# A block of linear attention and SwiGLU: the outputs' way back in halves, another round with one SwiGLU unit, centring a round later

## The chip, the cores and the metric

The kernel runs on one core of a Trainium2 chip. The metric is the device time of one execution in microseconds. Several executions give a median; one more was recorded by the hardware profiler, and all engine and queue times below are from that one.

The core has five engines, each with its own instruction queue in order: TensorE (PE in the profile, its weight loads PEld), VectorE (DVE), ScalarE (ACT), GpSimd (POOL) and SyncE (SP). In this kernel SP issues every DMA, so SP's queue decides when each transfer starts. PSUM, where TensorE leaves its results, has eight banks; here six turn in a ring and two form one pair.

## The reference

```python
xn = layernorm(x)                                   # x: 2048 tokens x 640, bf16
q, k, v = split(xn @ wqkv)                          # 32 heads of 20
pq, pk = q @ w_phi, k @ w_phi                       # per head
phi_q = concat(softmax(pq), softmax(-pq))           # 40 features per head
phi_k = concat(softmax(pk), softmax(-pk))
kv, z = phi_k^T @ v, sum over tokens of phi_k       # per head
o = (phi_q @ kv) / (phi_q @ z + 1e-6)
out = x + o @ wo + (silu(xn @ w1) * (xn @ w3)) @ w2 # SwiGLU width 1536
```

`kv` and `z` are sums over all tokens, so K's stage must be complete before any `o` can be made.

## The kernel before

The tokens are 16 tiles of 128, and four groups of four tiles. The program's order is written out by hand and kept; each engine takes its instructions in that order.

**First stage (to about 58 us).** Tiles are loaded, normalized and transposed into `xnT` (features on partitions, tokens along), weights are loaded, `w_phi` is multiplied into the K and Q projections (`fuse`), and `v` is computed (`vaug`). For the first four tiles (`RAW = 4`) v is computed from x that is not centred; it is corrected later: `column_sum` (L334, ScalarE) sums the columns of v's weights, the sums go out to `row` in DRAM and come back on all partitions (`less_sum`, in the tile `wide`), and `raw_centred` (L342, VectorE) adds drift times sum to `v_raw` and writes `vaug`.

**K's stage.** A loop of 16 rounds over the tiles, the four uncentred ones last. A round has `phi_unit` (TensorE's `pk`; exponentials on ScalarE; row sums L422 and reciprocals L424 on VectorE; the product L425 on GpSimd), `kv_unit` for the tile of two rounds before (TensorE's `pkv`), and one or two SwiGLU units from a list (`fill`: `gp` and `up` on TensorE, a tanh on ScalarE, the products L489 and L492 on VectorE, into `hT`). The condition on `i` names the rounds with one unit. Rounds 4 to 8 also have a `fuse` and a `column_sum`; round 9 issues `row` and `less_sum`; rounds 10 to 13 have a `raw_centred`.

**Q's stage.** A loop of 20 rounds `t`. Rounds 0 to 15 have `phi_unit` for Q (`pq`), and `phi_transposed(t)` (L528) issues the DMA transpose of its phi into one of two buffers. Two rounds later `r_unit(t - 2)` (L537, `pr`) multiplies it by `kv`, VectorE divides (L553 to L558), and `o_transposed` (L583) issues the DMA transpose of the result. Rounds 0 to 6 fill with the rest of the SwiGLU units.

The output of groups 0 to 2 is made transposed: `out_piece(g, c)` makes 128 features for 512 tokens (12 matmuls L642 and 5 L647, one bank), and VectorE adds x transposed (L650) and writes `yTs[g % 2]`. `x_back(t)` (L632) issues the DMA transpose of a tile of x from DRAM for it, into `xTs[g]`; groups 0 and 2 share one buffer. `group_back(g)` (L656) transposes a group's output by DMA into the only buffer `y`, and `group_stored(g)` stores `y`. The last group's four tiles are made the other way round, with tokens on partitions (`out_unit`, L600; 34 matmuls for a tile, and for the last tile two parts of 17); each takes a row block of x (`residual`, two buffers `xr`), adds it (L609) and stores the result.

In each round of Q's loop SP is given, in this order: what `out_unit` and `residual` issue, `o_transposed`, `phi_transposed`, `group_back`, `group_stored`, `x_back`. In round 12 all engines also load a flag (L974) that chooses whether a safe second computation follows; here it does not run. SP waits at each of its instructions until what this one needs is there, and all behind it wait with it.

Of the kernel before, what the change touches and what calls it, by code (L numbers as in the profile page):

```python
# [8 lines left out]
P = 128  # L9
# [3 lines left out]
def kernel(  # L13
# [33 lines left out]
    RAW = 4  # L47
# [12 lines left out]
    out2 = out[0]  # L60
# [6 lines left out]
    def bank(name, dt=f32):  # L67
        n = 512 if dt == f32 else 1024
        return psum.tile([P, n], dt, name=name, tag="bank")

    def pair(name):
# [43 lines left out]
    yTs = [  # L115
        a.rearrange("p (t c s) -> p t c s", t=4, c=KD)
        for a in (flat1[:, 0:G], flat3[:, 2 * G : 3 * G])
    ]
    y = flat1[:, G : 2 * G].rearrange("p (t c s) -> p t c s", t=4, c=KD)
# [25 lines left out]
    def ld(dst, src):  # L145
        nc.sync.dma_start(out=dst, in_=src)
# [9 lines left out]
    with tc.manual_schedule():  # L156
# [18 lines left out]
        for c in range(KD):  # L175
# [15 lines left out]
            out=mask[:], in_=mask[:], pattern=[[-20, LH]], base=0,  # L191
# [3 lines left out]
            out=mask[:], in_=mask[:], pattern=[[20, LH]], base=19,  # L195
# [7 lines left out]
            out=own[:], in_=own[:], pattern=[[-64, 2], [-20, 3]], base=0,  # L203
# [3 lines left out]
            out=own[:], in_=own[:], pattern=[[64, 2], [20, 3]], base=19,  # L207
# [124 lines left out]
        def column_sum(c):  # L332
            junk = work.tile([P, D], bf, name="junk")
            nc.scalar.activation(  # L334
                out=junk[:], in_=wvT[:, c], func=AF.Identity, scale=-1.0,
                accum_out=sums[:, c : c + 1],
            )

        def raw_centred(t):
            for c0, n, k in ((0, 10, 60), (10, 1, 40)):  # L340
                cols = slice(60 * c0, 60 * c0 + k * n)
                nc.vector.scalar_tensor_tensor(  # L342
                    out=vaug[:, t, c0 : c0 + n, 1 : 1 + k],
                    in0=less_sum[:, cols].rearrange("p (c e) -> p c e", c=n),
                    scalar=drift[:, t : t + 1],
                    in1=v_raw[:, t, cols].rearrange("p (c e) -> p c e", c=n),
                    op0=ALU.mult, op1=ALU.add,
                )

        def tile_of(t):  # L350
            return slice(t * P, (t + 1) * P)
# [61 lines left out]
        def phi_unit(t, w, name, exps=exps, cols=None):  # L413

            ps = by_token(cols or tile_of(t), w, name, CH)
            dst = phi[:, t % 4]
            exps(ps, dst)
            rows = dst.rearrange("p c g f -> p (c g) f")[:, :, 0:60].rearrange(
                "p a (i d) -> p a i d", d=Dh
            )  # L420
            sk = work.tile([P, 2 * NCH, 3], f32, name="sk")
            nc.vector.reduce_sum(out=sk[:], in_=rows, axis=AX.X)  # L422
            rk = work.tile([P, 2 * NCH, 3], f32, name="rk")
            nc.vector.reciprocal(out=rk[:], in_=sk[:])  # L424
            nc.gpsimd.tensor_mul(  # L425
                out=rows, in0=rows, in1=rk[:, :, :, None].to_broadcast([P, 2 * NCH, 3, Dh])
            )
# [12 lines left out]
        def fuse(dst, wT, d, ps, copy=None):  # L440

            for c in range(NF):
                b, i = divmod(c, 3)
                h0 = 4 if c == NF - 1 else 0
                nc.tensor.matmul(
                    ps[b][:, FR * i : FR * i + Dh * (LH - h0)],
                    wT[0:FR, c, d * P : (d + 1) * P],
                    wphi[0:FR, c, h0:LH],
                    start=(i == 0),
                    stop=(i == 2),  # L450
                    skip_group_check=True,
                )
            nc.scalar.copy(out=dst[:, d, 0:CH], in_=ps[0][:, 0:CH])
            (copy or nc.scalar.copy)(out=dst[:, d, CH:D], in_=ps[1][:, 0 : D - CH])
# [43 lines left out]
        def kv_unit(t, v1, acc, first, last):  # L498

            for c in range(NCH):  # L500
                b, i = divmod(c, 6)
                nc.tensor.matmul(  # L502
                    acc[:, b, VC * i : VC * i + 1 + Dh * HC[c]],
                    phi[:, t % 4, c].rearrange("p g f -> p (g f)"),
                    v1[:, c, 0 : 1 + Dh * HC[c]],
                    start=(first and i == 0),
                    stop=last,
                    skip_group_check=True,
                )
# [120 lines left out]
        def x_back(t):  # L630
            g, j = divmod(t, 4)
            nc.sync.dma_start_transpose(  # L632
                out=xTs[g][:, :, j * P : (j + 1) * P], in_=x2[tile_of(t), :]
            )
# [17 lines left out]
                in1=xTs[g][:, c].rearrange("p (t s) -> p t s", t=4), op=ALU.add,  # L652
            )

        def group_back(g):
            nc.sync.dma_start_transpose(  # L656
                out=y.rearrange("p t c s -> p (t c) s"),
                in_=yTs[g % 2].rearrange("p t c s -> p (t c s)"),
            )

        def group_stored(g):
            rows = out2[4 * g * P : 4 * (g + 1) * P, :]
            ld(rows.rearrange("(t p) d -> p t d", p=P), y.rearrange("p t c s -> p t (c s)"))

        norms = one.tile([P, 8], f32, name="norms")
        flag = one.tile([P, 1], mybir.dt.int32, name="flag")
# [25 lines left out]
        def fill(n):  # L692
            for _ in range(n):
                glu_unit(*glu.pop(0))()
# [200 lines left out]
        for i, t in enumerate(turns):  # L895
            phi_unit(t, wkphi, "pk")
            if i > 1:
                kv_unit(turns[i - 2], vaug[:, turns[i - 2]], acc, i == 2, False)
            if i and i not in (2, 3, 6, 9, 14, 15):
                fill(1)  # L900
            if 4 <= i < 9:
                fuse(wqphi, wqT, i - 4, [bank("pf"), bank("pf")])
            fill(1)
            if i == 0:
                nc.sync.dma_start_transpose(out=wvT, in_=A_wqkv[:, 2 * D : 3 * D])
            if 4 <= i < 9:
                column_sum(i - 4)
            if i == 9:
                ld(row[:].rearrange("c p -> p c"), sums[:])
                ld(less_sum, row[:].rearrange("c p -> (c p)").partition_broadcast(P))  # L910
            if 10 <= i < 10 + RAW:
                raw_centred(i - 10)
            if i >= 12:
                norm_unit(wkphi, 0, i - 12)
        ld(wo, A_wo.rearrange("(c p) d -> p c d", p=P))
# [1 line left out]


        pieces = {7 + i: [divmod(i, KD)] for i in range(9)}
        pieces.update({16: [(1, 4), (2, 0)], 17: [(2, 1), (2, 2)], 18: [(2, 3), (2, 4)]})  # L920
        xrs = {}
        for t in range(NST + 4):
            if t < NST:
                phi_unit(t, wqphi, "pq")
            if t < 2:
                kv_unit(turns[t - 2], vaug[:, turns[t - 2]], acc, False, t == 1)
                if t == 1:
                    kv_done([acc[:, 0], acc[:, 1]])
                    ld(w2, B_w2.rearrange("(c p) d -> p c d", p=P))
            if t < 7:  # L930
                (fill_halves(2, 2) if t < 6 else fill(1))
                fill(1)
            for g, c in pieces.get(t, []):
                out_piece(g, c)
            if t in (16, 17):
                xrs[t - 4] = residual(tile_of(t - 4))
            outs = {18: (12,), 19: (13, 14, 15)}.get(t, ())
            for j in outs:
                last = tile_of(j) if j == NST - 1 else None
                res = out_unit(hT[:, j], tile_of(j % 4), xrs[j], last)  # L940
                if j == 12:
                    group_back(2)
                if j == 13:
                    group_stored(2)
                if j < 14:
                    xrs[j + 2] = residual(tile_of(j + 2))
                if last is None:
                    ld(out2[tile_of(j), :], res[:])
            if 2 <= t < NST + 2:
                r_unit(t - 2)  # L950
                o_transposed(t - 2, (t - 2) // 4)
            if t < NST:
                phi_transposed(t)
            if t in (11, 16):
                group_back(t // 5 - 2)
            if t in (12, 17):
                group_stored(t // 5 - 2)
            if 2 <= t < 6:
                x_back(t - 2)
            if 7 <= t < 15:  # L960
                x_back(t - 3)
            if t < 4:
                norm_unit(wqphi, 1, t)
            if t == 4:
                ld(listed[:], norms[:])
                ld(flat, listed[:].rearrange("p g -> (p g)").partition_broadcast(1))
            if t == 10:
                flag_unit()
            if t == 12:
                ok = nc.values_load(flag[0:1, 0:1], min_val=0, max_val=1)  # L970
# [3 lines left out]
    with tc.If(ok == 0):  # L974
# [14 lines left out]
        with tc.For_i(0, NST, 1) as t:  # L989
            rows = bass.ds(t * P, P)  # L990
# [35 lines left out]
```

## Time and profile before

| what | us |
|---|---|
| median of 3 executions | 271.57 (271.52 to 272.26) |
| the profiled execution's own time | 270.82 |
| its span | 269.1 |
| TensorE busy | 261.1 (97%) |
| VectorE busy | 193.4 (72%) |
| ScalarE busy | 114.4 (43%) |
| GpSimd busy | 91.1 (34%) |

The profiled execution is 0.75 us below the median. A line of the profile's order of time gives start and length in us, engine, source line, operation, tile written <- tiles read, and how many instructions were merged; in brackets stands how long the engine was idle before it, and what ended that. "Busy" counts modelled ends of pipelined matmuls, so a gap between two starts, held against the same gap elsewhere, says more exactly what a wait cost. The program's names for tiles are used; `w` stands for w1 or w3 and for the buffers laid over them (`yTs`, `y`, most of `oTs`, `xTs[1]`), `reg_w` also for phi transposed, `reg_v` also for `w2` and one `oT`, `v_raw` also for `xTs[0]` and `xTs[2]`, `o__77` for `o_`.

### The profile page before, as it was taken

What the parts mean: (1) busy time and instruction counts of PE and PEld (TensorE: products, weight loads), DVE (VectorE), ACT (ScalarE), POOL (GpSimd) and SP (SyncE); (2) the same over time, 40 slices, a digit from 0 to 9 for tenths busy, and PEclk for the clock granted to TensorE, in tenths of its full rate; (3) what the DMA queues carried; (4) which work ended last, traced back from release to release, by engine and by line L of the source; (5) the groups of instructions that cost most, each with busy time, mean ns of one, the idle gap of its engine ahead of it and who ended that gap; (6) DMA issues with size and microseconds to landing.
All of it is one profiled execution on the core that took longest, in us unless ns stands there. A gap on an engine that the chain in (4) does not pass through costs nothing.

```text
span 269.1 us, 5001 instructions
## 1 busy us (share of the span) xinstructions
PE 261.1 (97%) x1842; PEld 154.6 (57%) x1868; DVE 193.4 (72%) x354; ACT 114.4 (43%) x348; POOL 91.1 (34%) x88
## 2 busy tenths in 40 slices
PE   8999999999999999899999999999999997999995
PEld 7766565655555555455665555555555553445763
DVE  4789984397876778599989999998899684342121
ACT  5875354745667654546766554324223320000000
POOL 4042520063633337054373333346336433000000
PEclk9999999999999999999999999999999999999999
DMA  6998857974000001500009545557766899473731
GB/s 187 254 248 192 111 118 210 294 146 87 0 0 2 1 3 6 166 2 0 2 0 282 121 107 120 84 130 155 127 155 71 191 203 173 104 145 124 182 110 55
DMA packets 83340, 31.41 MB, mean 117 GB/s; under 512 B 71791, under 2 KB 81903, under 8 KB 83312
## 3 DMA queue, kind: packets, MB, share of 16 engines
q1 hardware_dynamic: 83312, 31.05, 52.0%
q8 instruction: 16, 0.26, 0.4%
q14 instruction: 12, 0.10, 0.1%
HBM read 11.17 MB, written 2.63 MB: 51 GB/s over the span
## 4 chain that ended last, share of the span: by engine, by line
PE 87%; issue 4%; DMA 4%; DVE 3%; ACT 1%; SPq 0%; DVEq 0%
PE gp L461 14%; PE up L461 14%; PE acc L642 13%; PE pq L359 8%; PE acc L600 7%; PE pv L359 6%; PE pk L359 6%; PE acc L647 5%; PE gp L705 2%; PE up L705 2%; DMA wide<-row 2%; PE pr L537 2%; PE pv L316 2%; PE pkv L502 1%; DMA reg_w<-phi 1%
## 5 line engine op out<-in xcount | busy, mean ns | idle before, releaser
L425 POOL TENSOR_TENSOR phi<-phi,rk 128x1320 bf16<-128x1320 bf16 x32 | 77.2, 2412 | 108.8 <-DVE rk L424 87.3
L461 PEld LDWEIGHTS <-w 128*128 128x128 bf16 x400 | 37.8, 98 | 41.5 <-issue 1.0
L422 DVE TENSOR_REDUCE sk<-phi 128x66 f32<-128x1320 bf16 x32 | 48.8, 1524 | 17.3 <-ACT phi L388 16.2
L359 PEld LDWEIGHTS <-xnT 128*128 128x128 bf16 x440 | 41.7, 98 | 19.4 <-DMA xnT<-reg_h 0.6
L461 PE MATMUL gp<-xnT,w 128*128 128x512 bf16 x186 | 48.4, 378 | 1.5 <-DVE gs L489 0.9
L461 PE MATMUL up<-xnT,w 128*128 128x512 bf16 x197 | 49.5, 379 | 0.3
L388 ACT ACTIVATE phi<-pq 128x360 bf16<-128x360 f32 (+2 forms) x96 | 24.8, 366 | 42.4 <-issue 31.8
L642 PE MATMUL acc<-reg_h,reg_v 128*128 128x512 bf16 x180 | 41.3, 379 | 0.0
L472 ACT ACTIVATE th<-gp 128x512 f32<-128x512 f32 x47 | 28.6, 610 | 24.1 <-PE gp L461 18.8
L492 DVE SCALAR_TENSOR_TENSOR reg_h<-gs,up 128x512 bf16<-128x512 bf16 x47 | 32.3, 688 | 4.8
L489 DVE SCALAR_TENSOR_TENSOR gs<-th,gp 128x512 bf16<-128x512 f32 x47 | 30.8, 655 | 4.4 <-ACT th L472 4.4
L388 ACT ACTIVATE phi<-pk 128x360 bf16<-128x360 f32 (+2 forms) x96 | 24.9, 370 | 19.7 <-PE pk L359 19.7
L642 PEld LDWEIGHTS <-reg_v 128*128 128x128 bf16 x180 | 17.4, 98 | 19.1
L359 PE MATMUL pk<-wkphi,xnT 128*128 128x360 bf16 (+1 forms) x160 | 24.3, 299 | 0.0
L359 PE MATMUL pq<-wqphi,xnT 128*128 128x360 bf16 (+1 forms) x160 | 24.3, 299 | 0.0
L424 DVE RECIPROCAL rk<-sk 128x66 f32<-128x66 f32 x32 | 18.1, 566 | 3.2
L359 PE MATMUL pv<-reg_w,xnT 128*128 128x360 bf16 x120 | 17.4, 299 | 0.0
L245 DVE BATCH_NORM_STATS2 st<-reg_h 128x6 f32<-128x320 bf16 x32 | 13.4, 478 | 3.9 <-DMA reg_h<-in_A_x_dram 3.9
L650 DVE TENSOR_TENSOR w<-acc,v_raw 128x512 bf16<-128x512 f32 x10 | 6.7, 672 | 12.6 <-PE acc L647 9.6
L558 DVE TENSOR_TENSOR o__77<-pr,den 128x360 bf16<-128x360 f32 (+1 forms) x32 | 14.2, 486 | 0.6
L374 ACT CAST reg_v<-pv 128x360 bf16<-128x360 f32 (+2 forms) x36 | 9.8, 349 | 11.1 <-PE pv L359 11.1
L609 DVE TENSOR_TENSOR res<-acc,xr 128x320 bf16<-128x320 f32 (+2 forms) x8 | 3.6, 487 | 14.6 <-PE acc L600 14.6
(92 smaller groups left out, 235.8 us busy)
## 6 DMA issues: line engine op xcount, KB each, us to landing
w<-in_B_w_dram SPq DMA_DIRECT2D x2, 1280.0 KB, 6.1
reg_h<-in_A_x_dram SPq DMA_DIRECT2D x6, 320.0 KB, 4.7
reg_v<-in_B_w_dram SPq DMA_DIRECT2D x1, 1920.0 KB, 8.5
out_dram<-w SPq DMA_DIRECT2D x3, 640.0 KB, 3.5
w<-in_B_w_dram SPq DMA_DIRECT2D x4, 320.0 KB, 4.6
reg_w<-in_A_wqkv_dram SPq DMA_DIRECT2D x5, 160.0 KB, 3.2
reg_w<-in_A_wo_dram SPq DMA_DIRECT2D x1, 800.0 KB, 7.4
reg_h<-in_A_x_dram SPq DMA_DIRECT2D x4, 160.0 KB, 3.7
```

The lines of the kernel that those rows point to most:

```text
L359: nc.tensor.matmul(ps[i][:, 0 : b - a], xnT[:, c, cols], w[:, c, a:b], start=(c == 0), stop=(c == KD - 1), skip_group_check=True,)
L388: nc.scalar.activation(out=dst[:, c0 : c0 + n, g, 0:k], in_=p.rearrange("p (c f) -> p c f", c=n), func=AF.Exp, scale=1.0 - 2.0 * g,)
L422: nc.vector.reduce_sum(out=sk[:], in_=rows, axis=AX.X)
L424: nc.vector.reciprocal(out=rk[:], in_=sk[:])
L425: nc.gpsimd.tensor_mul(out=rows, in0=rows, in1=rk[:, :, :, None].to_broadcast([P, 2 * NCH, 3, Dh]))
L461: nc.tensor.matmul(ps, w[:, c, fi * P : (fi + 1) * P], xnT[:, c, sc * 512 : (sc + 1) * 512], start=(c == 0), stop=(c == KD - 1),)
L472: nc.scalar.activation(out=th[:], in_=gp, func=AF.Tanh, scale=0.5)
L489: nc.vector.scalar_tensor_tensor(out=gs[:], in0=th[:], scalar=1.0, in1=gp, op0=ALU.add, op1=ALU.mult)
L492: nc.vector.scalar_tensor_tensor(out=hT[:, 4 * sc : 4 * sc + 4, fi, :], in0=gs[:].rearrange("p (t s) -> p t s", t=4), scalar=0.5, in1=up.r ...
L558: nc.vector.tensor_mul(out=o_[:, t % 2, Dh * h0 : Dh * h1].rearrange("p (h d) -> p h d", d=Dh), in0=p3[:, :, 0:20], in1=den[:, h0:h1, None ...
L600: nc.tensor.matmul(ps[:, 0 : b - a], rows[j][0], rows[j][1][:, a:b], start=(j == 0), stop=(j == len(rows) - 1),)
L642: nc.tensor.matmul(acc4, w2[:, k, cols], hT[:, 4 * g : 4 * g + 4, k, :], start=(k == 0), stop=False,)
```

## The change

- In K's stage round 7 has one SwiGLU unit instead of round 9; the units keep their order. `raw_centred` moves from rounds 10 to 13 to rounds 11 to 14.
- `group_back` and `group_stored` take a half (two tiles of a group), so three transposes and three stores become six each. Group 0's halves go back in rounds 11 and 12 and are stored in 12 and 13; group 1's go back in 16 and 17, and are stored in 17 and 18; group 2's go back in 18 and are stored in 19.
- Piece (2, 0) moves from round 16 to 17, piece (2, 2) from 17 to 18.
- `x_back` of tiles 8 to 11 moves from rounds 11 to 14 to rounds 13 to 16.

```diff
-        def group_back(g):
+        def group_back(g, i):
+            two = slice(2 * i, 2 * i + 2)
             nc.sync.dma_start_transpose(
-                out=y.rearrange("p t c s -> p (t c) s"),
-                in_=yTs[g % 2].rearrange("p t c s -> p (t c s)"),
-            )
-
-        def group_stored(g):
-            rows = out2[4 * g * P : 4 * (g + 1) * P, :]
-            ld(rows.rearrange("(t p) d -> p t d", p=P), y.rearrange("p t c s -> p t (c s)"))
+                out=y[:, two].rearrange("p t c s -> p (t c) s"),
+                in_=yTs[g % 2][:, two].rearrange("p t c s -> p (t c s)"),
+            )
+
+        def group_stored(g, i):
+            rows = out2[(4 * g + 2 * i) * P : (4 * g + 2 * i + 2) * P, :]
+            ld(
+                rows.rearrange("(t p) d -> p t d", p=P),
+                y[:, 2 * i : 2 * i + 2].rearrange("p t c s -> p t (c s)"),
+            )
...
-            if i and i not in (2, 3, 6, 9, 14, 15):
+            if i and i not in (2, 3, 6, 7, 14, 15):
                 fill(1)
...
-            if 10 <= i < 10 + RAW:
-                raw_centred(i - 10)
+            if 11 <= i < 11 + RAW:
+                raw_centred(i - 11)
...
-        pieces.update({16: [(1, 4), (2, 0)], 17: [(2, 1), (2, 2)], 18: [(2, 3), (2, 4)]})
+        pieces.update({16: [(1, 4)], 17: [(2, 0), (2, 1)], 18: [(2, 2), (2, 3), (2, 4)]})
+        backs = {11: (0, 0), 12: (0, 1), 16: (1, 0), 17: (1, 1)}
...
                 if j == 12:
-                    group_back(2)
+                    group_stored(1, 1)
+                    group_back(2, 0)
+                    group_back(2, 1)
                 if j == 13:
-                    group_stored(2)
+                    group_stored(2, 0)
+                    group_stored(2, 1)
...
-            if t in (11, 16):
-                group_back(t // 5 - 2)
-            if t in (12, 17):
-                group_stored(t // 5 - 2)
+            if t in backs:
+                group_back(*backs[t])
+            if t in (12, 13):
+                group_stored(0, t - 12)
+            if t == 17:
+                group_stored(1, 0)
             if 2 <= t < 6:
                 x_back(t - 2)
-            if 7 <= t < 15:
+            if 7 <= t < 11:
                 x_back(t - 3)
+            if 13 <= t < 17:
+                x_back(t - 5)
```

## The prediction

> **What bounds the kernel now.** I read the page's busy shares first, then what TensorE waited for, then its order of time around those waits, then the queue of DMA issues (SP's) that one of them leads to.
>
> ```profile
> span 269.1 us, 5001 instructions
> PE 261.1 (97%) x1842; PEld 154.6 (57%) x1868; DVE 193.4 (72%) x354; ACT 114.4 (43%) x348; POOL 91.1 (34%) x88
> PEclk9999999999999999999999999999999999999999
> PE 87%; issue 4%; DMA 4%; DVE 3%; ACT 1%; SPq 0%; DVEq 0%
> ```
>
> TensorE is busy for 97% of the span at the full granted clock. The change adds and removes no matmul, so only time in which TensorE stands still can be won or lost. What it waited for:
>
> ```profile
> PE pr L537 <- DMA reg_w<-phi: 1.6, 1, 1.6
> PE gp L461 <- DVE gs L489: 0.9, 1, 0.9
> PE idle L223 <- PEq L1010: 0.8, 1, 0.8
> ```
>
> The third is at the program's start, which nothing here touches. TensorE's order of time at the other two (start, length, operation):
>
> ```profile
> 111.54 1.52 PE L359 MATMUL pk<-wkphi,xnT 128*128 128x360 bf16 x10
> 112.90 0.49 PE L502 MATMUL pkv<-reg_v,phi 128*128 128x61 bf16 x11
> 114.26 1.24 PE L461 MATMUL gp<-xnT,w 128*128 128x512 bf16 x5 [0.87 <-DVE gs L489]
> 118.57 1.52 PE L359 MATMUL pk<-wkphi,xnT 128*128 128x360 bf16 x10
> ...
> 213.33 2.75 PE L642 MATMUL acc<-reg_h,reg_v 128*128 128x512 bf16 x12
> 215.92 1.24 PE L647 MATMUL acc<-w,reg_w 128*128 128x512 bf16 x5
> 217.00 0.50 PE L537 MATMUL pr<-kvr,reg_w 128*128 128x63 bf16 x11
> 217.34 1.52 PE L359 MATMUL pq<-wqphi,xnT 128*128 128x360 bf16 x10
> 218.70 2.75 PE L642 MATMUL acc<-reg_h,reg_v 128*128 128x512 bf16 x12
> 221.50 1.03 PE L647 MATMUL acc<-w,reg_w 128*128 128x512 bf16 x4
> 224.12 0.51 PE L537 MATMUL pr<-kvr,reg_w 128*128 128x63 bf16 x11 [1.59 <-DMA reg_w<-phi]
> ```
>
> The starts give the full price. K's round 12 lasts 118.57 - 111.54 = 7.03 us, where its neighbours with two units last 6.00 and 6.01: 1.03 lost. In Q's stage a piece starts 3.67 before the `pr` behind it (213.33 to 217.00); the one at 218.70 should be followed at 222.37, and is at 224.12: 1.75 lost. Together 2.78. The trace's windows show some 0.1 idle per 15 us elsewhere after the first 30 us, and 3.3 from TensorE's last matmul to the end, so little else can be won.
>
> The first stall's cause, from VectorE's order of time, and the second's, from SP's:
>
> ```profile
> 106.85 0.69 DVE L492 SCALAR_TENSOR_TENSOR reg_h<-gs,up 128x512 bf16<-128x512 bf16 x1
> 110.54 1.02 DVE L342 SCALAR_TENSOR_TENSOR reg_v<-wide,drift,v_raw 128x600 bf16<-128x600 f32 x2 [3.00 <-DMA wide<-row]
> ```
>
> ```profile
> 207.06 3.95 SPq L656 DMA_TRANSPOSE w<-w  x1
> 211.05 1.28 SPq L632 DMA_TRANSPOSE v_raw<-in_A_x_dram  x1
> 212.44 1.21 SPq L583 DMA_TRANSPOSE w<-o__77  x1
> 213.82 1.34 SPq L528 DMA_TRANSPOSE reg_w<-phi  x1
> 215.21 0.58 SPq L146 DMA_DIRECT2D out_dram<-w  x1
> 215.84 1.93 SPq L632 DMA_TRANSPOSE v_raw<-in_A_x_dram  x1
> 218.99 1.21 SPq L583 DMA_TRANSPOSE w<-o__77  x1
> 220.31 1.49 SPq L528 DMA_TRANSPOSE reg_w<-phi  x1
> ```
>
> VectorE stands for 3.00 us in the first centring; the products behind it free PSUM banks late. On SP, group 0's way back holds the queue for 3.95, and x for group 2 (1.28 and 1.93) and the flag's load (217.77 to 218.99) follow, so round 13's phi is issued at 220.31 and lands at 224.1, when `pr` is already due.
>
> **The change part by part.** Times are on the clock of before; what the first part wins moves everything behind it alike.
>
> *Unit of round 7 to round 9.* Ten matmuls (2.16), a tanh (0.60) and two products (0.63 and 0.69) go two rounds on; no DMA. TensorE's sum is the same. Column sums end 2.16 earlier, so the list of sums is issued at 94.0 instead of 96.15 and its broadcast lands near 108.4 instead of 110.5. Rounds 6 and 7 then both have one unit. Round 7's gate starts at 85.08, in a bank that round 6's product leaves at 84.79: 0.3 to spare, so the cost lies between 0 and some 0.3, and I take 0. It can't be a gain, as TensorE has no gap there.
>
> *Centring one round later.* Four times two VectorE operations, 1.02 together, move from rounds 10-13 to 11-14. Round 11's reduction starts 6.00 after round 10's at 102.62, and its products end 4.92 later, at 113.5: the sums are there 3.0 to 5.1 before. The 3.00 wait goes, and with it 1.03 of TensorE. What is late next: a round with two products and a centring costs VectorE 5.77 (111.47 to 117.23) against TensorE's 6.01, so it keeps up; round 14, with one unit and a centring, costs about 4.4 against 3.85, and it falls 0.5 behind, won back in round 15 (3.43 against 3.85). The first reduction of Q's stage then starts about 3.2 after its `pq`, where it was 3.36 (135.63 - 132.27), and there VectorE did not stop TensorE. The products of K by v that read the centred tiles come in round 14 at the earliest. Cost 0.
>
> *Way back in halves.* The trace has no transpose of 10 blocks on SP. Its bounds are 1.37 for 11 blocks (phi) and 3.95 for the dearest of 20; 5 blocks cost 1.20, so the size hardly counts up to 11. I take 1.6, half of the median 3.16. It lands 3.1 (phi) to 6.3 (the slowest whole one) after issue. A store in halves costs SP 0.40 to 0.58 each, as whole ones do, and lands after 2.2 (160 KB) to 3.5 (640 KB). In all three transposes and three stores are added; by the row 3 x 0.55 for the stores, and for the transposes 6 x 1.6 against 3.95 + 3.16 + 2.98, about nothing.
>
> The Trainium skill, page "DMA: Bandwidth & Descriptors", sections "Anatomy of one DMA" and "Rules for kernel authors", speaks against such a split: one transfer costs about 2.0 us fixed plus its bytes at 436 GB/s, and many small ones should be coalesced. By that a 640 KB store takes 3.5, as the trace's median of 3.5 has it, and two halves 2.75 each, an estimate from the page. It is time to landing; if it were paid in series the six added transfers would cost 12 us.
>
> *SP's queue, round by round.* Round 11: o 204.31, phi 205.67, half back 207.06 to 208.7. Round 12: o at 208.7 (VectorE ended it at 208.63), phi 210.05, half back 211.45, half store 213.1 (its half has landed unless it took over 6.0), the flag's load 1.22, until 214.9. Round 13: o 214.9, phi 216.2 instead of 220.31. With the landing of 3.1 to 5.6 that this transpose has, it is there at 219.3 to 221.8; `pr` is due at 222.37. The 1.75 goes. Behind it half store 217.6, x of tile 8 at 218.2. Round 14: o 219.5, phi 220.8, landing 223.9 to 226.4.
>
> *Pieces later.* One of group 2's pieces (3.67) leaves round 16 and comes in 18, so round 16's `pr` is due at 222.37 + 0.36 + 3.67 = 226.4 instead of 231.81. Round 14's phi above is there with 0 to 2.5 to spare: this is the tightest place. Round 15's phi goes at 226.1 and lands by 231.7; its `pr` is due at 234.1.
>
> *x of group 2 later.* Tiles 8 to 11 go at 218.2, 222.2, 227.5 and 232.2; the last was at 226.01 and lands now at 235 to 236.2. Piece (2,0) leaves TensorE at 230.4, so VectorE waits in its addition for some 5 us. Behind it stand the addition of (2,1) and the last quotient, done near 238 to 239; SP's o of tile 15 and the half back behind it wait for that. Tile 15 of o is read after 256, and (2,0)'s bank is wanted again at 245.5 by the first output tile. Price 0, with over 8 us to spare.
>
> *The end of SP's queue.* Half back (1,1) near 240.3, its store when it has landed (245.2 to 246.6), half back (2,1) when that store has read y (248.8 to 250.2), its store at 254 to 256.5, then x of tile 15, which waited for 257.39 before and can go at 256 to 257, and is there 2.5 later; the last addition wants it at 262.2. Price 0. The matmuls' end moves by the sum alone, and the 3.3 behind it stay.
>
> **Sum.** 1.03 + 1.75 + nothing = 2.78 less. The profiled execution took 270.82, so 268.04; the median of the three runs is 271.57, 0.75 above it, and gives 268.8.
>
> **The rivals.** *Halves as dear as wholes.* If each half holds SP for 3.95, the second half runs to 217.7, phi of round 13 goes at 220.8 and lands near 224.5 (2.1 lost instead of 1.75), and round 14's, at 225.4, costs `pr` another 0.6. K's 1.03 covers 0.95 of that: 271.5, no change. For it: 20 blocks took more than twice 11. Against it: 5 to 11 blocks cost only 0.17 more. By that the rule of the Trainium skill in "DMA: Bandwidth & Descriptors", that small transfers are to be coalesced, would decide.
>
> *One stall stays in part.* Round 14's phi lands 1 us late in round 16, or VectorE's lag in K's stage is not gone: half to two thirds of the sum, 269.6 to 270.6. For it: the 0 to 2.5 to spare. Against it: the usual landing of 3.1 lies at the good end.
>
> *Slower: the chain of waits at SP's end.* Four steps now wait for the landing of the one before: half back (1,1), its store, half back (2,1), its store, and x of the last tile stands behind them all. A delay of that x counts from 262.2 + 1.3, since the second part's matmuls (1.85) cover all but the 0.56 of the first addition. To be 0.81 slower than before, 3.6 must be lost, so x must land at 267.1 and go at 264.6, 8 us later than worked out: the three landings between, 14.7 in my sum, would have to be over half as long again, and each us more is one lost: at 10 us more 273.5. The slowest whole way back took 6.3, and DMA's share there is about 0.6. It is possible only if the halves hinder each other.
>
> **How the numbers follow.** Both stalls gone: 0.75, at 268.8, with 268.0 to 269.5 as its own range (268.0 is the profiled execution's own figure). One stays in part: 0.11. No change by dear halves: 0.06. Slower: 0.08. A change under 0.3% (0.8 us) can't be told from none here. Faster is 0.75 + 0.11, same 0.06, slower 0.08. The range leaves out the last two and a little at the bottom: 268.0 to 270.8.
>
> **What would show it.** In TensorE's waits both lines gone, and K's round 12 at 6.0. On VectorE no wait at the first centring, and one of some 5 us in the first addition of group 2. On SP halves of 1.4 to 2.0, and round 13's phi issued at least 3 us earlier against its `pr`. Wrong it would be if halves take 3 or more, if `pr` of round 16 waits, if x of tile 15 is issued after its matmuls, or if a product in round 7 stops TensorE.

## The result, and the profile after

The changed kernel takes 269.94 us (median of 6 executions, 269.29 to 270.30), the kernel before 272.34 (6 executions, the three of the table above among them): a ratio of 0.9917, with a 95% interval of 0.9897 to 0.9938. The change makes it faster, clear of the noise, by less than 1%. By the ratio that is 2.3 us less, where 2.8 was forecast. The profiled execution took 269.29 (span 267.6), 1.53 less than the profiled one of before.

The changed kernel's page, its busy shares, and what TensorE waited for:

```profile
span 267.6 us, 5009 instructions
PE 260.6 (97%) x1842; PEld 154.4 (58%) x1868; DVE 194.7 (73%) x354; ACT 114.2 (43%) x348; POOL 91.1 (34%) x88
```

```profile
PE pr L537 <- DMA reg_w<-phi: 1.0, 1, 1.0
PE idle L223 <- PEq L1022: 0.8, 1, 0.8
PE pv L316 <- ACT reg_w L309: 0.3, 1, 0.3
PE pv L359 <- DMA xnT<-reg_h: 0.3, 1, 0.3
```

The wait for VectorE is gone. One wait of `pr` for its phi is still there, but TensorE's order of time shows that it is another one:

```profile
111.84 1.52 PE L359 MATMUL pk<-wkphi,xnT 128*128 128x360 bf16 x10
113.19 0.49 PE L502 MATMUL pkv<-reg_v,phi 128*128 128x61 bf16 x11
113.53 1.24 PE L461 MATMUL gp<-xnT,w 128*128 128x512 bf16 x4
...
117.84 1.52 PE L359 MATMUL pk<-wkphi,xnT 128*128 128x360 bf16 x10
...
217.96 2.75 PE L642 MATMUL acc<-reg_h,reg_v 128*128 128x512 bf16 x12
220.77 1.03 PE L647 MATMUL acc<-w,reg_w 128*128 128x512 bf16 x4
221.63 0.50 PE L537 MATMUL pr<-kvr,reg_w 128*128 128x63 bf16 x11
221.98 2.75 PE L642 MATMUL acc<-reg_h,reg_v 128*128 128x512 bf16 x12
224.56 1.24 PE L647 MATMUL acc<-w,reg_w 128*128 128x512 bf16 x5
226.85 0.51 PE L537 MATMUL pr<-kvr,reg_w 128*128 128x63 bf16 x11 [1.04 <-DMA reg_w<-phi]
```

K's round 12 lasts 6.00 (111.84 to 117.84). In Q's round 15 `pr` follows its piece after 3.67, unhindered. In round 16, where one piece has left, `pr` is due at 221.98 + 3.67 = 225.65 and comes at 226.85: 1.20 lost, in the place that the prediction called the tightest. VectorE's order of time at the first and the last centring, then SP's (the first row is phi of round 11, the last but one phi of round 14):

```profile
113.15 0.69 DVE L492 SCALAR_TENSOR_TENSOR reg_h<-gs,up 128x512 bf16<-128x512 bf16 x1
113.76 1.01 DVE L342 SCALAR_TENSOR_TENSOR reg_v<-wide,drift,v_raw 128x600 bf16<-128x600 f32 x2
...
130.38 2.15 DVE L342 SCALAR_TENSOR_TENSOR reg_v<-wide,drift,v_raw 128x600 bf16<-128x600 f32 x2
```

```profile
204.94 2.52 SPq L528 DMA_TRANSPOSE reg_w<-phi  x1
207.50 1.43 SPq L657 DMA_TRANSPOSE w<-w  x1
...
211.94 1.40 SPq L657 DMA_TRANSPOSE w<-w  x1
...
216.70 1.35 SPq L528 DMA_TRANSPOSE reg_w<-phi  x1
...
218.74 1.56 SPq L632 DMA_TRANSPOSE v_raw<-in_A_x_dram  x1
220.41 1.22 SPq L583 DMA_TRANSPOSE reg_v<-o__77  x1
221.73 1.37 SPq L528 DMA_TRANSPOSE reg_w<-phi  x1
223.15 1.94 SPq L632 DMA_TRANSPOSE v_raw<-in_A_x_dram  x1
```

A half holds SP for 1.4. Round 13's phi goes at 216.70 instead of 220.31. Counted from Q's first `pq` (131.54 here, 132.27 before) that is 2.9 earlier, where the queue in the prediction had 4.1. Round 14's goes at 221.73 and takes 5.07 to land, where the usual is 3.1.

TensorE's starts account for the two profiled executions. Each column is the time between two marks:

| stretch | before | after |
|---|---|---|
| span's start to K's first `pk` | 49.49 | 49.78 |
| K's stage (to Q's first `pq`) | 82.78 | 81.76 |
| to `pq` of round 15 | 85.07 | 85.07 |
| to `pr` of round 15 | 6.78 | 5.02 |
| to `pr` of round 16 | 7.69 | 5.22 (one piece of 3.67 less) |
| to `pr` of round 17 | 7.68 | 7.69 |
| to the output tiles | 7.68 | 11.35 (this piece more) |
| output tiles | 18.64 | 18.64 |
| to the span's end | 3.31 | 3.06 |

So K won 1.02 and round 15 won 1.76; round 16 lost 1.20; the end won 0.25, and the first stage was 0.29 longer in this execution: 1.54 together. The first stage, which the change leaves alone, is the noise here: over all profiles of this study it ends between 49.35 and 51.02 on TensorE (not near 58 us, as the description of the kernel has it). That is why I read the experiments below by these stretches first, and by their times only as far as the intervals go.

### The profile page after: what moved, and what is told of

Its sections match the earlier page's. It is cut to its first block, busy times and chain, and to the rows that moved or that the text cites. A ratio compares the mean times of both kernels' runs of the same rounds, so it can differ in the third digit from the quotient of the medians.

```text
span 267.6 us, 5009 instructions
## 1 busy us (share of the span) xinstructions
PE 260.6 (97%) x1842; PEld 154.4 (58%) x1868; DVE 194.7 (73%) x354; ACT 114.2 (43%) x348; POOL 91.1 (34%) x88
## 5 line engine op out<-in xcount | busy, mean ns | idle before, releaser
L492 DVE SCALAR_TENSOR_TENSOR reg_h<-gs,up 128x512 bf16<-128x512 bf16 x47 | 32.3, 688 | 4.8
```

Source lines behind the costliest of these rows:

```text
L492: nc.vector.scalar_tensor_tensor(out=hT[:, 4 * sc : 4 * sc + 4, fi, :], in0=gs[:].rearrange("p (t s) -> p t s", t=4), scalar=0.5, in1=up.r ...
```

## The experiments

My theory was that SP's queue order and VectorE's wait are the whole story, so that K's part and Q's part add up, and that the new wait in round 16 comes with Q's part. The rivals: the new wait comes only through K's shift; the halves are the cure and not x's place; the wait is one of the queue's order, or one of something that slows the transfer itself.

**K's part alone** (one unit in round 7, centring later; Q's stage as before).

```diff
-            if i and i not in (2, 3, 6, 9, 14, 15):
+            if i and i not in (2, 3, 6, 7, 14, 15):
-            if 10 <= i < 10 + RAW:
-                raw_centred(i - 10)
+            if 11 <= i < 11 + RAW:
+                raw_centred(i - 11)
```

> The kernel before with the two edits of K's stage alone (one unit in round 7 instead of 9, centring in rounds 11 to 14). If the stall at the first centring was all that these edits take away, K's round 12 lasts 6.0 instead of 7.03 us, the wait of `pr` in Q's round 15 stays at 1.6 to 1.8, and the time falls by about 1.0. If VectorE's lag (in the changed kernel Q's first reduction starts 4.3 us after its pq, not 3.2) costs TensorE anything in Q's first rounds, the gain is smaller and new waits for VectorE show there.

Ratio to before 0.9951 (0.9934 to 0.9968). K's stage lasts 81.76 and round 12 6.01: 1.02 won, as in the whole change. `pr` of round 15 still waits: it comes 6.49 after the `pq` (5.02 without a wait), so 1.47 is lost, a little under the 1.6 to 1.8 expected. No wait for VectorE shows. Round 14's `pr` comes 3.95 after its piece's start instead of 3.67: that phi had landed just in time before, and now lost 0.28, as the whole way back ahead of it held SP for 4.31 instead of 3.95.

**Q's part alone** is the changed kernel with the two edits above undone.

```diff
-            if i and i not in (2, 3, 6, 7, 14, 15):
+            if i and i not in (2, 3, 6, 9, 14, 15):
-            if 11 <= i < 11 + RAW:
-                raw_centred(i - 11)
+            if 10 <= i < 10 + RAW:
+                raw_centred(i - 10)
```

> The kernel before with the edits of Q's stage alone (halves, x of group 2 later, pieces later). If the parts are independent, the wait of `pr` in Q's round 15 goes (1.75 us won), the wait in round 16 that the changed kernel shows is there (1.0 to 1.2 lost), K's round 12 stays at 7.0, and the time falls by about 0.5. If the new wait comes only by the shift that K's part brings, it is not there and the time falls by 1.7.

Ratio 0.9962 (0.9947 to 0.9977). K's round 12 lasts 7.06. Round 15's wait is gone (5.02), and round 16 loses 0.52 (4.53, where 4.01 is without a wait), half of the 1.0 to 1.2 expected. The parts are independent, and the new wait belongs to Q's.

**One edit of K's part at a time.** The round of one unit moved to 7, centring as before:

```diff
-            if i and i not in (2, 3, 6, 9, 14, 15):
+            if i and i not in (2, 3, 6, 7, 14, 15):
```

> The kernel before with only the round of one unit moved from 9 to 7; centring in rounds 10 to 13 as before. The column sums go out 1.9 us earlier (94.3 instead of 96.2, as in the changed kernel), so VectorE's wait of 3.0 at the first centring falls to about 1, and if TensorE's banks give it that much, the stall of 1.03 goes as a whole: 1.0 less. If any wait there is passed on to TensorE, some 0.3 to 0.6 of it stays.

And only the centring a round later:

```diff
-            if 10 <= i < 10 + RAW:
-                raw_centred(i - 10)
+            if 11 <= i < 11 + RAW:
+                raw_centred(i - 11)
```

> The kernel before with only the centring one round later; the round of one unit stays 9. The sums land near 110.5, the first centring comes near 113.5: no wait, 1.0 less, so that either edit of K's stage would be enough alone. The last centring falls in round 14 with GpSimd's product beside it (in the changed kernel it took 2.15 instead of 1.01 us there); if that lag reaches TensorE the gain is smaller.

Ratios 0.9964 (0.9949 to 0.9980) and 0.9965 (0.9953 to 0.9978); K's stage lasts 81.76 in both. Either is enough. VectorE with the round moved:

```profile
108.62 1.02 DVE L342 SCALAR_TENSOR_TENSOR reg_v<-wide,drift,v_raw 128x600 bf16<-128x600 f32 x2 [0.68 <-DMA wide<-row]
```

It still waits 0.68 for the sums, where it was 3.00, and TensorE shows no wait for VectorE.

**x of group 2 later, without halves** (whole ways back and stores at their old places, K's stage as before). The pieces have to move too: otherwise VectorE's addition of round 16 would wait for an x that SP issues behind what waits for VectorE.

```diff
-        pieces.update({16: [(1, 4), (2, 0)], 17: [(2, 1), (2, 2)], 18: [(2, 3), (2, 4)]})
+        pieces.update({16: [(1, 4)], 17: [(2, 0), (2, 1)], 18: [(2, 2), (2, 3), (2, 4)]})
-            if 7 <= t < 15:
+            if 7 <= t < 11:
                 x_back(t - 3)
+            if 13 <= t < 17:
+                x_back(t - 5)
```

> The kernel before with x of group 2 two rounds later and the pieces one round later (without which VectorE would wait for an x that stands behind it in SP's queue), but whole ways back and whole stores, K's stage as before. If it is x's two transposes ahead of round 13's phi that made it late, that phi is issued near 217 instead of 220.3 and its wait goes, as with halves: 1.3 to 1.7 less, or 0.5 if the wait in round 16 comes too. If it is the 3.9 us hold of the whole way back, the wait stays above 1 and nothing is won.

**Halves alone**: the changed kernel's `group_back`, `group_stored` and their rounds, with x, pieces and K's stage as before. Against the kernel before, the calls are:

```diff
+        backs = {11: (0, 0), 12: (0, 1), 16: (1, 0), 17: (1, 1)}
...
                 if j == 12:
-                    group_back(2)
+                    group_stored(1, 1)
+                    group_back(2, 0)
+                    group_back(2, 1)
                 if j == 13:
-                    group_stored(2)
+                    group_stored(2, 0)
+                    group_stored(2, 1)
...
-            if t in (11, 16):
-                group_back(t // 5 - 2)
-            if t in (12, 17):
-                group_stored(t // 5 - 2)
+            if t in backs:
+                group_back(*backs[t])
+            if t in (12, 13):
+                group_stored(0, t - 12)
+            if t == 17:
+                group_stored(1, 0)
```

> The kernel before with the ways back and stores in halves over two rounds alone; x of group 2 and the pieces as before. By the queue worked out with 1.4 per half, round 13's phi is issued near 218.9 instead of 220.3 and lands at 222 to 224, so its wait of 1.75 falls to 0 to 1.0; round 16's pr has 3.7 us more and does not wait. Time 0.7 to 1.7 less. If the halves alone are the cure, the whole 1.75 goes; if x's place is, nearly nothing does.

Ratios 0.9926 (0.9904 to 0.9949) and 0.9938 (0.9919 to 0.9957). With x later, round 15 takes 5.02 and round 16 4.01: no wait of `pr` at all. With the halves, round 15 takes 5.47, so 0.45 of the 1.76 stays, and round 16 has its piece and does not wait. SP's issue of round 13's phi, first with the halves alone, then with x later:

```profile
219.70 1.39 SPq L528 DMA_TRANSPOSE reg_w<-phi  x1
```

```profile
218.16 1.36 SPq L528 DMA_TRANSPOSE reg_w<-phi  x1
```

The second is of an execution whose Q stage began 1.16 later (133.44 against 132.28). So by these two profiles x's place is the stronger half of the cure, and the halves do most of it alone; either expectation's extreme ("only the one") was wrong. The times don't tell the two apart, as their intervals overlap.

**K's edits and x later, without halves.** To see whether the changed kernel needs the halves at all; the edits of K's part and of x above together.

> The changed kernel without the halves: K's edits, x of group 2 and the pieces later, but whole ways back and whole stores at their old places. If the order on SP decides and the halves are not needed, the waits of `pr` in rounds 15 and 16 are both under 0.3 us, TensorE's order from K's stage to the end is that of the kernel with x of tile 8 behind the phi (1.0 + 1.76 less than before), and the time is 2.5 to 2.8 below before. If the halves are needed, the wait in round 15 or 16 is 0.5 or more.

268.56 us, ratio 0.9906 (0.9884 to 0.9927). Rounds 15 and 16 take 5.02 and 4.01, K's stage 81.76: no wait is left between K's first matmul and the end. The halves are not needed, though it is close: round 14's phi goes out 88.98 after Q's first `pq`, takes 4.82 and lands at 225.50, 0.30 before its `pr` starts. What the halves add is at the end, 3.32 here against 3.06.

**x of tile 8 behind round 14's phi** (all else as changed).

```diff
             if t < NST:
                 phi_transposed(t)
+            if t == 14:
+                x_back(8)
...
-            if 13 <= t < 17:
+            if 14 <= t < 17:
                 x_back(t - 5)
```

> The changed kernel with x of tile 8 issued behind round 14's phi instead of a round earlier. If the new wait in round 16 comes from what stands ahead of that phi on SP, the phi is issued near 220.1 instead of 221.7, lands by 224.8 even if it takes 5 us, and the wait of 1.0 to 1.2 goes: 1.0 to 1.2 less than the changed kernel, 3.5 less than before. If only the instruction packet at 222.6, which stops the transposes for 1.5 to 2 us, makes it late, and it hits this phi all the same, it lands about 1.9 later than usual but still in time, with the same gain; a gain under 0.5 would speak against both.

268.24 us, ratio 0.9898 (0.9872 to 0.9923): 2.8 less than before, where 3.5 was expected, and by the ratios 0.5 less than the changed kernel, where 1.0 to 1.2 was. SP (its last row is x of tiles 8 and 9 together) and TensorE at the place:

```profile
218.27 1.22 SPq L583 DMA_TRANSPOSE reg_v<-o__77  x1
219.66 1.37 SPq L528 DMA_TRANSPOSE reg_w<-phi  x1
221.06 3.74 SPq L632 DMA_TRANSPOSE v_raw<-in_A_x_dram  x2
```

```profile
221.59 2.75 PE L642 MATMUL acc<-reg_h,reg_v 128*128 128x512 bf16 x12
224.17 1.24 PE L647 MATMUL acc<-w,reg_w 128*128 128x512 bf16 x5
225.25 0.50 PE L537 MATMUL pr<-kvr,reg_w 128*128 128x63 bf16 x11
```

The phi still takes 4.93 to land (at 224.59), but it is there when `pr` is due, at 225.25. No wait of `pr` is left in TensorE's list.

**What slows that transfer.** In the changed kernel, the DMA view of the 2 us from 222.5 to 224.5 (forty slices of 0.05 us; then packets by queue, MB, share of the 16 engines):

```profile
GB/s 15 20 343 0 0 0 0 0 31 97 189 251 276 266 271 276 271 276 236 92 26 0 0 0 0 0 0 0 0 0 10 5 10 5 10 10 10 10 10 10
q1 hardware_dynamic: 530, 0.14, 115.3%
q8 instruction: 1, 0.02, 4.4%
```

One packet of instructions starts there (the 343 in the third slice), and from about 223.5 the transposes all but stand: 0 to 26 GB/s for a whole microsecond. In the trace's list of packets those of queue 8 have 16384 bytes and come every 230 to 270 TensorE instructions from 82 us on (but for the last), so they come at nearly the same place of the work in every execution: this one 91.1 to 91.6 us after Q's first `pq` in both profiles of the changed kernel, in Q's part alone and in both with x of tile 8 behind the phi, the one in round 11 at 74.0 to 74.3. To move them against the work, the warming matmuls at the start are made fewer and longer:

```diff
-        nought = one.tile([P, P], bf, name="nought")
+        nought = one.tile([P, 512], bf, name="nought")
...
-                nc.tensor.matmul(idle[:, 0:P], nought[:], nought[:])
+                nc.tensor.matmul(idle[:], nought[:, 0:P], nought[:])
```

with `WARM` 5 instead of 20, and `warm(1)` instead of `warm(4)`: as many columns, 36 TensorE instructions fewer ahead of all others.

> The changed kernel with TensorE's 24 warming matmuls of 128 columns as 6 of 512: as much work at the start, but 36 TensorE instructions fewer ahead of everything. TensorE's instruction packets of 16 KB come every 256 instructions or so (17 us), so they come some 2.4 us later against the work: near 225.0 instead of 222.6. If such a packet is what made round 14's phi land after 5.07 instead of 3.1, it now lands after 3.1 to 3.9, the wait of `pr` in round 16 goes, and the time falls by about 1.2. If SP's queue order alone makes it late, the wait of 1.0 and the time stay. What changes in the first 5 us at the start (TensorE's clock comes up with the same work) is expected under 0.3.

The packet comes at 226.43, 93.7 after Q's first `pq`: 2.1 to 2.6 later, as its count said. SP's order is the same, round 14's phi goes at 221.90, and lands after 3.44 instead of 5.07. TensorE does not wait:

```profile
223.16 2.75 PE L642 MATMUL acc<-reg_h,reg_v 128*128 128x512 bf16 x12
225.74 1.24 PE L647 MATMUL acc<-w,reg_w 128*128 128x512 bf16 x5
226.82 0.50 PE L537 MATMUL pr<-kvr,reg_w 128*128 128x63 bf16 x11
```

Instead the packet hits the next phi, which holds SP for 2.69 and lands after 4.98, with time to spare. It is the landing that shows the packet's part; the missing wait alone would not. The packet of round 11 has moved too, and round 14's phi goes out 89.2 after Q's first `pq`, 1.0 sooner than in the changed kernel's first profile, so a landing of 5.07 would have cost no more than 0.2 here. The expected fall of 1.2 in the time did not come: 269.43 us, ratio 0.9943 (0.9919 to 0.9968), against 0.9917 of the changed kernel. In its profile the first stage ends at 50.96, 1.2 later than in the changed kernel's, with a wait of 1.3 for `xnT` there, so the expectation of under 0.3 at the start was wrong, or this is that stage's own noise; one profile doesn't tell.

**The changed kernel and the better one again, side by side.**

> The changed kernel once more, beside the next one on the same chip. If the wait in round 16 is a matter of one execution, it is under 0.5 here; if it comes from an instruction packet that TensorE's count of instructions puts there, the packet starts 91.1 to 91.3 us after Q's first pq again and the wait is 0.5 to 1.2. Time 1.6 to 2.4 below before.

> The kernel with x of tile 8 behind round 14's phi once more. No wait of `pr` at all, 0.6 to 1.2 below the changed kernel and 2.8 to 3.2 below before; if its lead came from a lucky start (the first stage's length differs by 1.6 us between executions), it is level with the changed kernel here.

268.73 us, ratio 0.9918 (0.9897 to 0.9939), and 268.25 us, 0.9898 (0.9877 to 0.9919). In the changed kernel the packet came at 91.2 again and the phi took 5.02, but round 16 lost only 0.15, where 0.5 to 1.2 was expected with the packet there. The difference to the first profile is in SP's queue: there an earlier packet (205.64) fell on round 11's phi, which held SP for 2.52; here (206.43) it fell on the first half back, held for 1.98, and round 14's phi went out 89.2 after Q's first `pq` instead of 90.2. With x of tile 8 behind the phi there was no wait again. The intervals of the two overlap; the lead of 0.5 rests on the ratios of both pairs (0.9898 and 0.9898 against 0.9917 and 0.9918) and on the absence of the wait in the trace. It has the lowest ratio of this study, but its interval also overlaps that of K's edits and x later without halves (0.9906), measured beside it.

## Why the prediction was right, and where it was off

*What bounds the kernel, and the two stalls.* Both terms of the sum held: 1.03 forecast and 1.02 measured in K's stage, 1.75 and 1.76 in round 15, and each came with its own part alone. That starts, and not the idle figures (0.87 and 1.59), gave their sizes was confirmed to 0.01.

*Unit to round 7, centring later.* The cost of 0 held. They were forecast together and are two cures: either alone removes the 1.03. One step in it was off: the first reduction of Q's stage starts 4.34 after its `pq` (131.54 to 135.88), not 3.2. The last centring took 2.15 instead of 1.01, with GpSimd's product beside it. TensorE was not stopped.

*Halves.* 1.6 was taken between 1.37 and 3.95; in the changed kernel's first profile they hold SP for 1.34 to 1.51 and land after 3.4 to 3.7 (in others one that an instruction packet hits holds it for up to 2.64). The rival "halves as dear as wholes" is out. The fixed cost of about 2.0 us for each transfer, from the Trainium skill, page "DMA: Bandwidth & Descriptors", section "Anatomy of one DMA", is not paid in series here: the six added transfers cost SP its issues, and their landings run beside other work. That section is about transfers that GpSimd issues, while SP issues all of these. The page's advice to coalesce many small transfers, in "Rules for kernel authors", is neither borne out nor refuted: a half has 320 KB, where the page calls those under 64 KB mostly overhead, and whole ways back with x later left TensorE as free of waits as the best kernel with halves.

*Pieces later: the step that was mis-sized.* "0 to 2.5 to spare" was priced at 0, by the usual landing of 3.1 and by an issue of round 14's phi at 220.8, which is 88.53 after Q's first `pq`. Both were off. The landing is 4.7 to 5.2 in all seven profiles where the instruction packet falls 0.9 to 2.8 after the issue of this phi. The issue came 0.6 to 1.7 later than worked out, chiefly because another such packet holds SP for 0.6 to 1.2 longer in round 11. `pr` is due 94.11 after Q's first `pq`, so neither alone would have cost anything (88.53 + 5.07 = 93.60, and 90.19 + 3.1 = 93.29); the two together (90.19 + 5.07 = 95.26) did. Round 16 lost 1.20, 0.52 and 0.15 in three profiles. The bounds of the landing (3.1 to 5.6) held, and the choice at their good end did not; the issue times on SP had been given without bounds. The rows for the dear end were there: the same transpose took 4.97 in round 11 of before, and the whole way back that the packet hit there held SP for 3.95, the others for 3.15 and 2.98.

*The rivals.* What came is in the main the first half of "one stall stays in part", which named this place and 1 us and had a chance of 0.11: both old stalls went, and a new one took their place in part. The 269.94 lies in that rival's range (269.6 to 270.6) and above the 268.0 to 269.5 given for both stalls gone. The rival's upper end of 270.6 is too high by the prediction's own words: half to two thirds of the sum gives 269.7 to 270.2.

*x later, and SP's end.* Both priced at 0, and right. VectorE stood for 7.33 before the first addition of group 2; its piece left TensorE at 231.03 and the addition began at 236.28, so the wait for x of tile 11 is 5.3 of that, where some 5 was forecast, and it cost TensorE nothing. And x of the last tile went out at 256.10, over six us before the addition that reads it (262.70). The rival of the chain at SP's end is out.

*The sum against the times.* 268.8 was forecast, 269.94 and 268.73 measured in two sets of executions. Neither figure alone says how good the forecast was, as the kernel before moved as well: it was 271.57 when the forecast was made, 272.34 beside the 269.94 and 271.04 beside the 268.73. That 268.73 is so near to 268.8 is luck. The two kernels were 2.2 to 2.3 apart both times, where 2.78 was forecast: the sum less a part for round 16, within what the first stage's noise allows. The 0.25 won at the end, which the prediction left at 3.3, is in it too.

## What to carry to other kernels

When a busy engine is stopped at few places, price each stop by the distance between starts, held against the same distance in a neighbouring round. A change that takes work from between a transfer and its reader spends that transfer's slack: price it with the slowest landing and the latest issue that the trace shows, together, and not with the usual ones. If the order of a queue is free, put the transfer that is read next ahead of those that are read much later; here one `x_back` behind one phi was worth the wait that the whole change had left.

## What the runs showed of the hardware

DMA transposes come late where an instruction packet of 16 KB falls among them. Take the phis of all thirteen profiles, without Q's second one, which lands after 5.6 to 7.6 while `w2` is loaded. Of 51 that such a packet fell on, from 0.3 us before their issue to their landing, 48 landed after 3.77 to 5.61, and three, hit 2.5 us after their issue, after 3.06 to 3.09. The 130 others landed after 3.05 to 3.77. SP's issue of a phi takes 1.34 to 1.49, and up to 2.84 where the packet falls at its start. In the changed kernel the flow of data all but stands for a microsecond, as shown above. In the kernel before, from 206.5 to 208.5, the packet is in the 22nd slice, and the whole way back of group 0 (3.95) was held:

```profile
GB/s 0 0 0 0 0 0 5 72 164 256 256 271 261 276 266 276 256 159 51 10 0 328 0 0 0 0 0 0 0 0 0 0 0 0 0 0 0 0 0 5
q8 instruction: 1, 0.02, 3.0%
```

So a part of what I had taken for the price of 20 blocks was this packet. The flow had already dropped when the packet's record starts, and it also drops to nothing for 0.65 us between transposes that no packet hits (from 214.35 in the kernel before), so the landings tell more than the gaps. The Trainium skill, page "Runtime: NRT & Kernel Launch", section "Instruction fetch mechanics", says that instructions are fetched in blocks of 16 KiB, 256 instructions, and that this is mostly hidden. The trace agrees with the block and about with the count (230 to 270 recorded ones); it is not hidden from transposes. That the packet itself, and not something that comes with it, makes them late is not shown by a run; that moving it moves the delay is.

One operation of VectorE with both operands in SBUF took longer beside GpSimd. The centring of 600 columns took 834 to 845 ns alone, and 1977 with GpSimd's product around its start at 130.38:

```profile
129.30 2.41 POOL L425 TENSOR_TENSOR phi<-phi,rk 128x1320 bf16<-128x1320 bf16 x1 [3.59 <-PE pk L359]
```

The same place took 1976 to 1978 in all eight profiles in which the centring is moved, also where nothing else is. The product L492, which has one operand in SBUF and one in PSUM, took 686 to 690 ns in K's and Q's stages of every profile, with GpSimd's product beside it or without. The Trainium skill, page "SBUF — State Buffer", section "Who interferes with whom", has it so: with two SBUF inputs VectorE contends with a GpSimd instruction that reads SBUF, and the second to start blocks. The row and the page agree, and the prediction could have known it.

The end of the program is 0.25 shorter in all profiles with halves (3.06) than in all without (3.31 to 3.32), in thirteen profiles. SP's waits show where: only the kernels without halves have this one, at the program's last line (here of the kernel before).

```profile
SPq L1021 <- DMA out_dram<-res: 0.3, 1, 0.3
```

There SP goes through eight checks, one for each of the semaphores that its DMAs take in turn, 0.06 us apart when nothing is missing. Without halves there are 114 DMAs, the last store has the semaphore of the second check, and six checks still follow its landing. With the six more of the halves it has that of the eighth, and lands while the others are gone through. So this gain comes from the number of DMAs and not from anything that a half does; a run with the number alone changed was not made.
